# Head-pair attention of batch 0 in another engine order, with moved key-transpose slots, Sin table load, GpSimd squares and V load

## The chip, the cores and the metric

The kernel runs on one core of a Trainium2 chip. The metric is the device time of one execution in microseconds; of several executions the median is given. The core's engines are TensorE (PE in the profile; PEld is its weight load), VectorE (DVE), ScalarE (ACT), GpSimd (POOL) and SyncE (SP). Each works through its own list of instructions in order and waits on semaphores for the others.

## What is computed

Chunked attention, and behind it an MLP with a snake activation, over 4 batches of 768 rows, 8 heads of 64:

```
for c in range(24):                      # chunk 32, left 16, right 8
    k_full = concat(mem_k, k[max(0, 32c-16) : min(768, 32c+40)])   # 8 memory rows first; v likewise
    a = softmax(q_c @ k_full.T / 8)
    out[:, :, 32c:32c+32] = a @ v_full
x = out.transpose(0, 2, 1, 3).reshape(3072, 512)
h = x @ w_in                             # 512 -> 2048
g = h + sin(alpha * h)**2 / (alpha + 1e-09)
result = g @ w_out                       # 2048 -> 512
```

Inputs and output are float32; the kernel multiplies in bf16.

## The kernel before, in words

Three chunks make a window of 96 queries, whose scores are 128 rows of keys: a window's keys, 8 memory keys among them, lie side by side in `kTi`, and the same for values in `vws[b % 2]`. A batch has 8 windows and 4 head pairs, so 32 cells. A unit of attention takes 4 cells. Its steps are: scores (8 matmuls, L266, into a PSUM tile `sc`), exponentials with masks as bias on ACT (L279, into `pt`), PV (8 matmuls, L294, into `ot`), reciprocal and scaling on DVE (L298, L299, into `x_blk`), a transpose on PE (L309) and a copy into `xT` (L312).

For batches 1 to 3 (`burst`) a unit is one window of all head pairs. The last layer of the batch before, held in a generator (`Stream`, matmuls at L439), is woven between the steps. For batch 0 (`first_burst`) there is nothing to weave in, and a unit is half of the windows of one head pair: units 0 and 1 are pair 0, and so on. Its order is written by hand in the string `ORDER`: `k n` and `q n` transpose the keys and queries of pair n on PE (L241) and copy them to `kTi` (DVE, L246 and L252) and `qT` (L259: ACT for pairs 0 and 2, DVE for 1 and 3); `memk` and `memv` place memory keys and values of batch 0 (L147, L141); `s n` is scores and exponentials of unit n; `v n` PV and scaling; `x n` the transpose to `xT`; `z n` is n spin matmuls on zeros (L160), which also precede each transpose inside `turn`. Since every engine takes its instructions in program order, this string sets what each engine does next.

PSUM has eight banks here: three two-bank slots (`big`, for scores, PV and first-layer tiles) and two one-bank slots (`smp`, for spins, batch 0's transposes and second-layer outputs).

After the burst comes the first layer of the batch, 16 tiles `ft` of 128 features (`l1`): 8 matmuls (L382), Sin on ACT (L394, or L391 in two halves), a square, and a fused multiply and add on DVE into `gT` (L411, or L407 in halves). A string of 16 letters says which engine squares: A for ACT (L397), D for DVE (L403), P for GpSimd (L399). The square on DVE and the fused operation of a tile are issued after the next tile's preparations (`finish`). In batch 0 tiles 3, 7 and 11 are split tiles: they use the one-bank slots, so that more tiles are in flight.

Exp and Sin need different tables on ACT, so each change between attention and first layer loads one (ACT_TABLE_LOAD).

GpSimd also issues the loads (q, k, v, weights; they cast to bf16), and copies each head pair of the next batch together (`pair_up`, L215, tile `pr`) for its transposes (L238); in batch 0 some of these copies are DVE's. Batch 1's values are loaded (`load_v(1, ...)`, four issues, L138) from within batch 0's first layer, and its pairs are transposed after it, three matmuls of the last layer between two transposes.

The memory values come as f32 in `memv_f`, once for all batches, and are cast once on ACT (L189) into `memv_st`; `put_memv(b)` copies batch b's to all windows (L141).

Of the kernel before, what the change touches and what calls it, by code (L numbers as in the profile page):

```python
# [11 lines left out]
NEG = -30000.0  # L12
KW = 856
ORDER = (
    "k 0,q 0,memk 0,k 1,s 0,q 1,s 1,memv 0,s 2,k 2,v 0,q 2,s 3,x 0,v 1,k 3,s 4,x 1,q 3,s 5,"
    "z 1,v 2,s 6,x 2,z 1,v 3,s 7,x 3,z 2,v 4,z 2,v 5,x 4,z 1,v 6,x 5,z 1,v 7,x 6,z 1,x 7"
)
BF = mybir.dt.bfloat16
F32 = mybir.dt.float32
# [30 lines left out]
def kernel(  # L50
# [45 lines left out]
    memkT = consts.tile([P, HP, 32], BF, name="memkT")  # L96
    memv_st = consts.tile([P, B, H, D], BF, name="memv_st")
    memk_f = gp.tile([32, H, D], F32, name="memk_f", tag="gT")
    memv_f = gp.tile([P, B, H, D], F32, name="memv_f", tag="gT")
    w_in_sb = consts.tile([P, KT, d_ff], BF, name="w_in_sb")  # L100
    w_out_sb = consts.tile([P, FT, d_model], BF, name="w_out_sb")
    alpha_sb = consts.tile([P, FT], F32, name="alpha_sb")
# [35 lines left out]
            nc.gpsimd.dma_start(dst, src)  # L138

    def put_memv(b):  # L140
        nc.vector.tensor_copy(  # L141
            vws[b % 2][64:72, :, :, 0:D],
            memv_st[64:72, b].unsqueeze(2).to_broadcast([NM, H, NJ, D]),
        )
# [41 lines left out]
    nc.vector.tensor_scalar(  # L186
        out=biasm[:], in0=rows[:, 0:5], scalar1=1.0, scalar2=-NEG, op0=ALU.subtract, op1=ALU.mult)
    nc.scalar.copy(memk_bf[:], memk_f[:])
    nc.scalar.copy(memv_st[64:72], memv_f[64:72])  # L189
    for hp in range(1, HP):  # L190
        load_v(0, 16 * hp, 16 * hp + 16)
    with nc.allow_non_contiguous_dma(reason="alpha transpose load"):
# [32 lines left out]
            return smp.tile([P, 6, P], BF, name="tt_a", tag="sm")  # L225
        return big.tile([P, 6, P], BF, name="tt_b", tag="big")

    def turn(src, hp):

        if src.shape[1] == 6:  # L230
            t = t_tile()
        else:
            z = smp.tile([P, 512], F32, name="z", tag="sm")
            spin(2, z)
            t = z[:].bitcast(BF)[:, 0:6 * P].rearrange("p (r c) -> p r c", r=6)
        for r in range(6):
            if src.shape[1] == 6:
                nc.tensor.transpose(t[:, r, :], src[:, r].rearrange("p e d -> p (e d)"), ident[:])  # L238
            else:
                for e in range(2):  # L240
                    nc.tensor.transpose(t[64 * e:64 * e + 64, r, :], src[:, 2 * hp + e, r, :], ident[:])  # L241
        return t

    def t_k(kb, hp):
        t = turn(kb, hp)
        nc.vector.tensor_copy(  # L246
            kTi[:, hp, 72:72 + 7 * 104].rearrange("p (s c) -> p s c", c=104)[:, :, 0:96]
            .rearrange("p s (a r) -> p s a r", r=6),
            t[:, :, 8:120].rearrange("p r (s a) -> p s a r", a=16),
        )  # L250
        for t0, c0 in ((0, 16), (120, 800)):
            nc.vector.tensor_copy(  # L252
                kTi[:, hp, c0:c0 + 48].rearrange("p (a r) -> p a r", r=6),
                t[:, :, t0:t0 + 8].rearrange("p r a -> p a r"),
            )
# [2 lines left out]
        t = turn(qb, hp)  # L258
        copy(qT[:, hp, :].rearrange("p (a r) -> p a r", r=6), t[:, :, :].rearrange("p r a -> p a r"))  # L259

    def qk_exp(cells):

        sc = big.tile([P, 2, 512], F32, name="sc", tag="big")
        for c, (hp, j) in enumerate(cells):
            for e in range(2):
                nc.tensor.matmul(  # L266
                    sc[:, e, QW * c:QW * c + QW],
                    kTi[64 * e:64 * e + 64, hp, 104 * j:104 * j + P],
                    qT[64 * e:64 * e + 64, hp, QW * j:QW * j + QW],
                )  # L270
        pt = pts[state["n"] % NPT]
        state["n"] += 1
        for m in range(3):
            cols = [((1 if j == 0 else 0), 4, (2 if j == NJ - 1 else 3))[m] for _, j in cells]
            c0 = 0
            for c1 in range(1, 5):
                if c1 < 4 and cols[c1] == cols[c0]:
                    continue
                nc.scalar.activation(  # L279
                    pt[:, 0:H * QW].rearrange("p (g e c) -> p e g c", g=4, e=2)[:, :, c0:c1, 32 * m:32 * m + 32],  # L280
                    sc[:, :, 0:4 * QW].rearrange("p g (e c) -> p g e c", e=4)[:, :, c0:c1, 32 * m:32 * m + 32],
                    ACTF.Exp, bias=biasm[:, cols[c0]:cols[c0] + 1], scale=0.125,
                )
                c0 = c1
        return pt
# [28 lines left out]
    def row(j):  # L314
        return [(hp, j) for hp in range(HP)]

    def burst(b, stream, shares, lag):

        xT = xp.tile([P, KT, S], BF, name="xT")
        ptl, xbl = {}, {}  # L320
        for s in range(NJ + lag + 1):
            n = shares[s] if s < len(shares) else 0
            if s < NJ:
                ptl[s] = qk_exp(row(s))
            stream.take(n // 3, True)
            if 0 <= s - lag < NJ:
                xbl[s - lag] = pv(b, row(s - lag), ptl.pop(s - lag))
            stream.take((n + 1) // 3, True)
            if 0 <= s - lag - 1 < NJ:
                j = s - lag - 1  # L330
                xt(xT[:, :, QW * j:QW * j + QW], *xbl.pop(j))
            stream.take((n + 2) // 3, True)
        return xT

    def first_burst(kq):

        xT = xp.tile([P, KT, S], BF, name="xT")
        cells = [[(u // 2, 4 * (u % 2) + c) for c in range(4)] for u in range(8)]
        ptl, xbl = {}, {}
        for what, n in [t.split() for t in ORDER.split(",")]:  # L340
            n = int(n)
            if what == "k":
                t_k(kq[0], n)
            elif what == "q":
                t_q(kq[1], n, nc.vector.tensor_copy if n in (1, 3) else nc.scalar.copy)
            elif what == "memk":
                mt = smp.tile([P, HP, 32], BF, name="mt", tag="sm")
                for hp in range(HP):
                    nc.tensor.transpose(
                        mt[:, hp, :],  # L350
                        memk_bf[0:32, 2 * hp:2 * hp + 2, :].rearrange("p e d -> p (e d)"),
                        ident[0:32, 0:32])
                nc.vector.tensor_copy(memkT[:], mt[:])
                put_memk(0)
            elif what == "memv":
                put_memv(0)
            elif what == "s":
                ptl[n] = qk_exp(cells[n])
            elif what == "z":
                spin(n)  # L360
            elif what == "v":
                xbl[n] = pv(0, cells[n], ptl.pop(n))
            elif what == "x":
                hf = n % 2
                xt(xT[:, n // 2, HALF * hf:HALF * hf + HALF].rearrange("p (k c) -> p k c", k=KT),
                   *xbl.pop(n), nc.vector.tensor_copy if n < 4 else nc.scalar.copy)
        return xT
# [95 lines left out]
    for i in range(B):  # L463
        gT = gp.tile([P, FT, S], BF, name="gT")
        last = i == B - 1
        at_ft = {2 * n: n for n in range(8)}
        pieces = []
        if not last:
            srcs = [(kq_next[n % 2], n // 2) for n in range(2 * HP)]
        state["pools"] = 1  # L470

        def pair_to(n):
            while len(pieces) < min(n, 2 * HP):
                pieces.append(pair_up(*srcs[len(pieces)], nc.vector.tensor_copy if i == 0 and len(pieces) in (2, 4, 6) else None))

        def piece(n):
            pair_to(n + 3)
            (t_k if n % 2 == 0 else t_q)(pieces[n], n // 2)

        if 0 < i < B - 1:  # L480
            pair_to(2)
        finish = None
        for ft in range(FT):
            sq = ("ADAPADAPDADADAAA" if i == 0 else "ADAAPDADADAPADAD")[ft]
            if 1 <= ft:
                stream.take(3 if last else 2)
            if 0 < i < B - 1 and ft in at_ft:
                piece(at_ft[ft])
            if i == 0 and ft == 8:
                load_v(1, 0, H * NJ)  # L490
            if i == 0 and ft == 13:
                pair_to(2)
            if finish is not None:
                finish()
            finish = l1(i, ft, xT, gT, sq, i == 0 and ft in (3, 7, 11))
        finish()
        stream.add(l2(i, gT, last))
        if not last:
            if i == 0:
                state["pools"], state["t"] = 3, 0  # L500
                stream.take(4)
                for n in range(2 * HP):
                    piece(n)
                    stream.take(3, True)
                put_memv(1)
            if i + 2 < B:
                kq_next = load_qk(i + 2)
            if i == 0:
                xT = burst(i + 1, stream, (5, 5, 5, 4, 4, 4, 4, 4, 3, 3, 3, 3), 3)
            else:  # L510
                xT = burst(i + 1, stream, (16, 8, 6, 6, 6, 5, 5, 5, 5, 5), 1)
            if i + 2 < B:
                put_memk(i + 2)
            stream.take(3)
            if i + 2 < B:
                load_v(i + 2, 0, H * NJ)
                put_memv(i + 2)
# [31 lines left out]
```

## Time and profile before

| | us |
|---|---|
| median of 4 runs | 237.43 (236.72 to 237.66) |
| the profiled execution | 236.15 |
| its span | 234.3 |
| busy: PE / DVE / ACT / POOL | 215.9 / 160.2 / 153.2 / 71.6 |
| first-layer matmuls L382, x488 | 87.3 |
| last-layer matmuls L439, x343 | 93.1 |
| batch 0: first burst until the first first-layer matmul | 27.80 |
| batch 0: first Sin / last Sin of the first layer starts | 29.80 / 52.44 |
| batch 1: first scores / first PV | 61.95 / 67.02 |

Times within the profile count from the span's start. In the rows of busy tenths each digit is the busy share of one of 40 equal slices, and PEclk is the clock that TensorE was granted. In the lines of a timeline stand start, length (of one instruction, or of a merged run of them), engine, source line, operation, output<-input, shapes and count; in brackets, how long the engine was idle before it and what ended that. The ends of matmuls are modelled, and GpSimd's spans are rough.

### The profile page before, as it was taken

To read this page: it belongs to the slowest core of one execution; us is meant where nothing else is said; L and a number is where in the kernel's file an instruction comes from. 1 tells how busy PE (TensorE), PEld (TensorE's weight loads), DVE (VectorE), ACT (ScalarE), POOL (GpSimd) and SP (SyncE) were. 2 spreads that over 40 slices of the span, in tenths; PEclk is the share of its full clock that TensorE was granted. 3 is DMA by queue.
4 is the path that set the end of the run, shared out by engine and by line. 5 is a ranking of instruction groups with operands and counts; after the bars stand their busy time and mean duration, and the time that the engine had idled before them with its cause. 6 is when DMAs were issued, how large, how long until landed. Compare 5 with 4: busy or idle time off the path is not lost.

```text
span 234.3 us, 4546 instructions
## 1 busy us (share of the span) xinstructions
PE 215.9 (92%) x1802; PEld 121.7 (52%) x1831; DVE 160.2 (68%) x287; ACT 153.2 (65%) x244; POOL 71.6 (31%) x84
## 2 busy tenths in 40 slices
PE   7677899969999999998999999998999999899994
PEld 2344555535545565554455656564555555453453
DVE  5488658997847987988557698978566358775110
ACT  3679499875697297899664787779564676880000
POOL 8899603923942115138300115020000020010000
PEclk9999999999999999999999999999999999999999
DMA  7999999999999910019996101000111110101112
GB/s 83 150 174 114 168 205 205 207 192 104 146 222 168 109 45 0 0 49 141 184 154 98 45 0 48 0 8 36 48 48 45 45 49 0 45 0 48 64 71 90
DMA packets 52365, 21.13 MB, mean 90 GB/s; under 512 B 36344, under 2 KB 49400, under 8 KB 52344
## 3 DMA queue, kind: packets, MB, share of 16 engines
q0 software_dynamic: 46128, 14.41, 72.3%
q1 hardware_dynamic: 6216, 6.43, 9.4%
q8 instruction: 14, 0.23, 0.5%
q14 instruction: 7, 0.06, 0.1%
HBM read 28.93 MB, written 6.29 MB: 150 GB/s over the span
## 4 chain that ended last, share of the span: by engine, by line
PE 64%; DVE 17%; issue 7%; ACT 6%; DMA 2%; POOL 1%; POOLq 1%; DVEq 0%; ACTq 0%
PE o L439 30%; PE hT L382 20%; DVE gT L411 6%; PE sc L266 3%; DVE s L403 3%; ACT u L394 3%; DVE x_blk L299 3%; PE ot L294 3%; PE ot L309 2%; DMA q_bf<-in_q_dram 2%; PE tt_a L238 2%; ACT s L397 2%; PE o L428 1%; DVE kTi L246 1%; PE z L160 1%
## 5 line engine op out<-in xcount | busy, mean ns | idle before, releaser
L439 PE MATMUL o<-w_out_sb,gT 128*128 128x512 bf16 x343 | 93.1, 380 | 2.0 <-issue 0.5
L382 PE MATMUL hT<-xT,w_in_sb 128*128 128x384 bf16 x488 | 87.3, 326 | 4.4 <-DVE gT L411 4.2
L411 DVE SCALAR_TENSOR_TENSOR gT<-s,inv_alpha,hT 128x768 bf16<-128x768 f32 x61 | 60.9, 1013 | 24.7 <-ACT s L397 16.7
L394 ACT ACTIVATE u<-hT,alpha_sb 128x768 f32<-128x768 f32 x61 | 54.6, 897 | 25.0 <-PE hT L382 23.9
L382 PEld LDWEIGHTS <-w_in_sb 128*128 128x128 bf16 x512 | 49.3, 98 | 39.6 <-issue 5.9
L279 ACT ACTIVATE pt<-sc,biasm 128x256 bf16<-128x256 f32 (+2 forms) x104 | 39.2, 464 | 14.3 <-PE sc L266 14.0
L439 PEld LDWEIGHTS <-gT 128*128 128x128 bf16 x368 | 31.9, 98 | 26.3 <-DVE gT L411 1.2
L399 POOL TENSOR_TENSOR s<-u 128x768 f32<-128x768 f32 x8 | 11.7, 1465 | 83.5 <-ACT u L394 61.3
L397 ACT ACTIVATE s<-u 128x768 f32<-128x768 f32 x33 | 27.8, 843 | 1.0
L138 POOL DMA_DIRECT2D vw<-in_v_dram x28 | 24.6, 889 | 0.3 <-issue 0.2
L403 DVE TENSOR_TENSOR s<-u 128x768 f32<-128x768 f32 x23 | 23.8, 1037 | 0.6 <-ACT u L394 0.5
L299 DVE TENSOR_TENSOR x_blk<-ot,rinv 96x512 bf16<-96x512 f32 x32 | 22.0, 686 | 1.1
L215 POOL COPY pr<-q_bf 128x768 bf16<-128x768 bf16 x12 | 10.2, 853 | 40.6 <-PE tt_a L238 27.1
L446 DVE COPY o_sb<-o 128x512 f32<-128x512 f32 x12 | 8.3, 689 | 15.5 <-PE o L439 15.4
L448 ACT COPY o_sb<-o 128x512 f32<-128x512 f32 x11 | 6.4, 582 | 17.9 <-PE o L439 17.9
L298 DVE RECIPROCAL rinv<-ot 96x8 f32<-96x8 f32 x32 | 6.4, 201 | 16.1 <-PE ot L294 15.8
L294 PEld LDWEIGHTS <-pt 128*128 128x128 bf16 x256 | 12.0, 97 | 6.3 <-issue 1.3
L294 PE MATMUL ot<-vw,pt 128*128 128x65 bf16 x256 | 13.0, 193 | 0.6 <-DVE xT L312 0.5
L160 PE MATMUL z<-zeros 128*128 128x512 bf16 x31 | 11.1, 456 | 2.5 <-DVE zeros L153 1.2
L266 PEld LDWEIGHTS <-kTi 64*128 64x128 bf16 x256 | 6.8, 94 | 12.3 <-PE ot L309 5.5
L309 PE MATMUL ot<-ident,x_blk 96*128 96x96 bf16 x128 | 10.8, 207 | 2.5 <-DVE x_blk L299 2.3
L238 PEld LDWEIGHTS <-pr 128*128 128x128 bf16 x144 | 10.0, 98 | 5.9 <-DVE pr L215 0.8
(65 smaller groups left out, 155.4 us busy)
## 6 DMA issues: line engine op xcount, KB each, us to landing
out_dram<-o_sb SPq DMA_DIRECT2D x23, 256.0 KB, 2.2
k_bf<-in_k_dram POOLq DMA_DIRECT2D x3, 768.0 KB, 7.6
q_bf<-in_q_dram POOLq DMA_DIRECT2D x3, 768.0 KB, 11.4
vw<-in_v_dram POOLq DMA_DIRECT2D x6, 384.0 KB, 15.6
w_out_sb<-in_moe_w_out_dram POOLq DMA_DIRECT2D x2, 1024.0 KB, 24.5
w_in_sb<-in_moe_w_in_dram POOLq DMA_DIRECT2D x3, 512.0 KB, 9.8
k_bf<-in_k_dram POOLq DMA_DIRECT2D x4, 192.0 KB, 5.1
q_bf<-in_q_dram POOLq DMA_DIRECT2D x4, 192.0 KB, 5.3
```

The lines of the kernel that those rows point to most:

```text
L138: nc.gpsimd.dma_start(dst, src)
L238: nc.tensor.transpose(t[:, r, :], src[:, r].rearrange("p e d -> p (e d)"), ident[:])
L279: nc.scalar.activation(pt[:, 0:H * QW].rearrange("p (g e c) -> p e g c", g=4, e=2)[:, :, c0:c1, 32 * m:32 * m + 32], sc[:, :, 0:4 * QW].re ...
L294: nc.tensor.matmul(otv[:, n // 4, n % 4, :], pt[:, QW * n:QW * n + P], vws[b % 2][:, 2 * hp + n % 2, j, 0:D + 1])
L299: nc.vector.tensor_tensor(out=x_blk[:].rearrange("p (g e) d -> p g e d", g=2), in0=otv[0:QW, :, :, 0:D], in1=rv.unsqueeze(3).to_broadcast( ...
L309: nc.tensor.transpose(xtp[:, kt, :], x_blk[:, 2 * kt:2 * kt + 2, :].rearrange("p e d -> p (e d)"), ident[0:QW, 0:QW])
L382: nc.tensor.matmul(hts[hf][:, 0:HALF], w_in_sb[:, kt, P * ft:P * ft + P], xT[:, kt, HALF * hf:HALF * hf + HALF], start=(kt == 0), stop=(kt ...
L394: nc.scalar.activation(u[:], hT[:, :, 0:HALF], ACTF.Sin, scale=alpha_sb[:, ft:ft + 1])
L397: nc.scalar.activation(s2[:], u[:], ACTF.Square)
L403: nc.vector.tensor_tensor(out=s2[:], in0=u[:], in1=u[:], op=ALU.mult)
L411: nc.vector.scalar_tensor_tensor(out=gv, in0=s2[:], scalar=inv_alpha[:, ft:ft + 1], in1=hT[:, :, 0:HALF], op0=ALU.mult, op1=ALU.add)
L439: nc.tensor.matmul(o[:], gT[:, ft, P * s:P * s + P], w_out_sb[:, ft, :], start=(ft == 0), stop=(ft == FT - 1),)
```

## The change

The order of the first burst is a new string, with scores (`s`) and exponentials (`e`) as separate steps. The memory values come straight after the memory keys; the second unit's scores no longer follow `q 1`; some spins go or move. The transposes of keys of pairs 0 and 1 use a two-bank slot; `turn` spins 3 times for pairs 0 and 1 and once for the others, instead of twice. The cast of memory values is per batch, on DVE for batch 0 and on ACT for the others, and `memv_f` has a buffer of its own. After the last exponentials of the burst a Sin of one column is issued, and the Sin table with it. In batch 0's first layer five squares change engine: 8 and 10 go from D to A, 9 from A to D, 11 and 14 from A to P. Batch 1's first two pair copies stand at tile 8 instead of 13, and the load of its values after the 16 tiles instead of at tile 8.

```diff
 ORDER = (
-    "k 0,q 0,memk 0,k 1,s 0,q 1,s 1,memv 0,s 2,k 2,v 0,q 2,s 3,x 0,v 1,k 3,s 4,x 1,q 3,s 5,"
-    "z 1,v 2,s 6,x 2,z 1,v 3,s 7,x 3,z 2,v 4,z 2,v 5,x 4,z 1,v 6,x 5,z 1,v 7,x 6,z 1,x 7"
+    "k 0,q 0,memk 0,memv 0,k 1,s 0,e 0,z 1,s 1,e 1,q 1,s 2,e 2,v 0,s 3,k 2,x 0,q 2,e 3,v 1,s 4,e 4,"
+    "k 3,x 1,q 3,s 5,e 5,v 2,z 1,s 6,e 6,x 2,v 3,z 1,s 7,e 7,x 3,z 1,v 4,z 1,v 5,x 4,z 1,v 6,x 5,z 1,v 7,x 6,z 1,x 7"
 )
...
-    memv_f = gp.tile([P, B, H, D], F32, name="memv_f", tag="gT")
+    memv_f = consts.tile([P, B, H, D], F32, name="memv_f")
...
     def put_memv(b):
+        (nc.vector.tensor_copy if b == 0 else nc.scalar.copy)(memv_st[64:72, b], memv_f[64:72, b])
         nc.vector.tensor_copy(
...
-    nc.scalar.copy(memv_st[64:72], memv_f[64:72])
...
-    def turn(src, hp):
+    def turn(src, hp, early=False):
...
-            z = smp.tile([P, 512], F32, name="z", tag="sm")
-            spin(2, z)
+            if early:
+                z = big.tile([P, 512], F32, name="zb", tag="big")
+            else:
+                z = smp.tile([P, 512], F32, name="z", tag="sm")
+            spin(3 if hp < 2 else 1, z)
...
-        t = turn(kb, hp)
+        t = turn(kb, hp, hp < 2)
...
             elif what == "s":
-                ptl[n] = qk_exp(cells[n])
+                scl[n] = qk(cells[n])
+            elif what == "e":
+                ptl[n] = exps(cells[n], scl.pop(n))
+                if n == 7:
+                    nc.scalar.activation(rows[:, 0:1], zeros[:, 0:1], ACTF.Sin)
...
-            sq = ("ADAPADAPDADADAAA" if i == 0 else "ADAAPDADADAPADAD")[ft]
+            sq = ("ADAPADAPADAPDAPA" if i == 0 else "ADAAPDADADAPADAD")[ft]
...
             if i == 0 and ft == 8:
-                load_v(1, 0, H * NJ)
-            if i == 0 and ft == 13:
                 pair_to(2)
...
         if not last:
             if i == 0:
+                load_v(1, 0, H * NJ)
                 state["pools"], state["t"] = 3, 0
```

`qk` and `exps` are the two halves of the former `qk_exp`, unchanged; `burst` calls one after the other.

More of the change, by code (lines that the diff above doesn't have):

```diff
@@ L259, in t_q, with qk @@
         copy(qT[:, hp, :].rearrange("p (a r) -> p a r", r=6), t[:, :, :].rearrange("p r a -> p a r"))
-    def qk_exp(cells):
+    def qk(cells):
         sc = big.tile([P, 2, 512], F32, name="sc", tag="big")
@@ L270, in qk_exp, with exps @@
                 )
+        return sc
+    def exps(cells, sc):
         pt = pts[state["n"] % NPT]
@@ L323, in burst @@
             if s < NJ:
-                ptl[s] = qk_exp(row(s))
+                ptl[s] = exps(row(s), qk(row(s)))
             stream.take(n // 3, True)
@@ L338, in first_burst @@
         cells = [[(u // 2, 4 * (u % 2) + c) for c in range(4)] for u in range(8)]
-        ptl, xbl = {}, {}
+        scl, ptl, xbl = {}, {}, {}
         for what, n in [t.split() for t in ORDER.split(",")]:
```

## The prediction

> **What bounds the kernel now.** I read the page's rows of busy tenths first, to see where an engine is not full. One column is 5.86 us.
>
> ```profile
> PE   7677899969999999998999999998999999899994
> DVE  5488658997847987988557698978566358775110
> ACT  3679499875697297899664787779564676880000
> POOL 8899603923942115138300115020000020010000
> PEclk9999999999999999999999999999999999999999
> ```
>
> From column 14 on TensorE is nearly full. In columns 1 to 5 (head-pair attention, to 27.8 us), no engine is full: there a chain of hand-overs sets the time. Columns 6 to 9 (first layer of batch 0) have PE, ACT and DVE all near full. The change works in these two stretches, so I took the timeline of them next.
>
> ```profile
> 6.84 1.89 ACT L189 CAST memv_st<-memv_f 8x2048 bf16<-8x2048 f32 x1 [1.28 <-DMA memv_f<-in_mem_v_dram]
> 8.57 0.50 DVE L147 COPY kTi<-memkT 128x256 bf16<-128x256 bf16 x1
> 8.76 0.80 ACT L259 COPY qT<-z 128x768 bf16<-128x768 bf16 x1
> ...
> 12.21 2.60 ACT L279 ACTIVATE pt<-sc,biasm 128x256 bf16<-128x256 f32 x8 [0.86 <-PE sc L266]
> ...
> 12.92 1.37 DVE L141 COPY vw<-memv_st 8x4096 bf16<-8x4096 bf16 x1
> ...
> 28.50 1.28 ACT L394 ACT_TABLE_LOAD   x1
> 29.80 0.90 ACT L394 ACTIVATE u<-hT,alpha_sb 128x768 f32<-128x768 f32 x1
> ...
> 50.94 1.46 PE L382 MATMUL hT<-xT,w_in_sb 128*128 128x384 bf16 x8 [1.57 <-DVE gT L411]
> ...
> 53.73 0.83 POOL L215 COPY pr<-q_bf 128x768 bf16<-128x768 bf16 x1 [5.55 <-PE tt_b L238]
> ...
> 61.54 2.07 DVE L141 COPY vw<-memv_st 8x4096 bf16<-8x4096 bf16 x1
> ...
> 62.22 1.28 ACT L279 ACT_TABLE_LOAD   x1
> ```
>
> The reader sees: ACT spends 1.89 us on memory values while the first query copy is ready (its transposes end at 8.09); the Sin table is loaded only when everything before it is done; the last first-layer tile waits 1.57 us for DVE; and the same memory-value copy costs 1.37 us once and 2.07 us another time.
>
> The profiled execution took 236.15 us: 234.3 of span and 1.85 around it. It is 0.5% under the runs' median of 237.43. I sum against the profile and carry the difference over.
>
> **1. The first burst.** ACT's 1.89 us copy goes: the first query copy starts at 8.1, not 8.76. The first scores (9.61) then wait for the k 1 transposes in front of them and start about 9.3. Their exps, 1.35 us, start at 9.7. The second scores now follow at once and no longer stand behind q 1, so their exps start at 11.05 instead of 12.21, 1.15 earlier.
>
> That is not the gain of the stage, because DVE gets more to do before k 1. Put_memk ends at 9.07. Then comes a copy of 8x512 values that no row shows: ACT's 32x512 cast of 0.62 bounds it above, DVE's 128x768 bf16 copy of 0.35 (55.17) below; I take 0.45, between, as it reads f32. Then the 8x4096 copy, 1.37 (1.22 to 2.07), the k 1 copies, 1.09 (9.68 to 10.77), and the q 1 copy, 0.96: 9.07 + 0.45 + 1.37 + 1.09 + 0.96 = 12.94. It ended at 12.89, so the third scores win nothing. PV 0 does: it stood behind k 2 (14.39) and now follows them, at 13.3. Its DVE result leaves about 1.7 us earlier, and from there the DVE work interleaves better. The last exps end near 23.0 instead of 23.63 (18.09 + 5.54): 0.6. Behind them, "z 2" becomes "z 1" twice; the second spin of a pair costs 0.60 - 0.38 = 0.22, one of the two hidden by waits for x_blk, so 0.2 to 0.4. The rest (PV, x_blk every 0.85, transpose, copy) keeps its length. hT starts at 26.9 instead of 27.80: **-0.9** (bounds -0.3 with the 2.07 copy and its followers, -1.3).
>
> The other parts cost nothing here. The extra spins before k 0 (0.4 at the cold 0.43 each) lie in the wait for q 0, 7.56, from which k 0 had over 1 us; without that cover they cost 0.4. The two-bank slots of k 0 and k 1 are free by the third scores (k 0's copies ended at 7.46). The DVE copies may hold up GpSimd's issues beside them (13.22 took 1.21 instead of 0.61). q 3 was issued at 10.18 and lands after a median of 5.3, at 15.5; its transposes come near 17.5, so 0.6 later is hidden. The values' own f32 buffer takes no one's place and adds no wait.
>
> **2. The table.** The eight hT matmuls end at 27.80 + 7 x 0.162 + 0.33 = 29.26, the table at 29.78: 0.54 was exposed. Now it is issued after the last exps, near 23.0, where ACT idled 1.71 before the first xT copy (25.34). With the dummy Sin (0.32, by the smallest exp) that is 1.60, and the copies wait for x_blk anyway. **-0.54**; if that idle time were gone, up to 1.28 would come back through the xT copies. [...] In the trace the ACTIVATE starts 1.30 after the load; I use the row.
>
> **3. Squares.** ACT loses one of 0.84 and DVE one of 0.95, GpSimd gains two of 1.47. Tile 11 is the costly one: its square takes 1.47 on GpSimd instead of 0.84 on ACT, and DVE's sum for tile 11 heads DVE's queue; behind it stand the square of 12 and the sums of 12 to 15, and the last hT waits for the sum of 12. u 11 ended at 45.66; 1.44 earlier by items 1 and 2 and 0.8 later by the square that ACT gains among 8 to 10 makes 45.0, the square 46.5. DVE has then sat idle for about 1.1 us, against the 0.95 of the one square fewer that it has by then. Tile 14 takes 0.6 longer but its sum is behind 12 and 13. I take **+0.2** (bounds -0.4, +0.8).
>
> [...]
>
> ```profile
> 84.30 0.83 POOL L215 COPY pr<-k_bf 128x768 bf16<-128x768 bf16 x1 [2.69 <-PE tt_a L238]
> 84.44 1.49 DVE L403 TENSOR_TENSOR s<-u 128x768 f32<-128x768 f32 x1
> ```
>
> A DVE square of 0.95 took 1.49. But under the two GpSimd squares of this stage (35.05, 40.31) lay only sums with one SBUF input, and these stayed 1.01. The new squares meet sums too. [...]
>
> **4. GpSimd's queue.** The V load of batch 1 (four issues, 41.72 to 46.0, 4.29 us) moves behind the square of 14. In front of it now stands that square's wait for u 14; behind it, the three q pair copies and the loads of batch 2. u 14 ended at 50.41; 1.44 earlier and 0.3 for what ACT no longer does makes 48.7, so square 14 ends near 50.2, the issues at 54.5, the q 1 pair at 55.3. Its transposes, at 56.58, would come 1.25 earlier, 55.3: just in time. Each further slip is paid one for one. **+0.1** (0 to +1.5). Landing: the issues took a median of 16.9 us to land, the last at 45.17 + 16.9 = 62.1, queued behind the second-layer weights; these still go first, so the V rows land near 62 to 64, before PV at 66.
>
> **5. Memory values per batch.** Batch 1's 8x512 copy, 0.62 by the nearest row, now stands on ACT between the last query copy and the Exp table (62.22). All exps move by it. PE had some 0.3 of slack there (the second PV at 68.54 starts as the fourth exps end), so **+0.35** (0 to 0.6). DVE waits for that copy; behind it stands nothing before 67.47. In batches 2 and 3 it lies in ACT's idle 4.42 and 1.22 us before u: nothing; without that cover 0.62 each.
>
> Sum: -0.9 - 0.54 + 0.2 + 0.1 + 0.35 = -0.79. The profile's 236.15 becomes 235.4, and the median 237.43 becomes 236.6.
>
> **Rivals.** A difference below 0.3% (0.7 us) can't be told from none.
> [...]
> - *GpSimd's queue becomes the bound: 238.2, slower.* If the V issues meet DVE copies as at 62.54 (2.02 instead of 1.34, so 0.7 each for the long ones), or square 14 is late, q 1's pair is ready 1.6 us late, TensorE stands still and -0.8 becomes +0.8. It decides once the pair copy ends more than 0.85 after 55.3. For: nothing covers that stretch. Against: in the same issues at 41.72 none was stretched.
> - *TensorE cools: 239.* Two spins fewer in all; if the clock fell in the burst, spins and matmuls double (0.43 instead of 0.215). The PEclk row shows no dip near it.
>
> **Chances.** Forecast 42%; returned by the lock, 33%; GpSimd's queue 20%; clock 5%. Faster 0.42, same 0.33, slower 0.25. The range goes from a front gain at its bound (237.43 - 1.6 = 235.8) to the queue rival with 0.1 beyond it, 238.3; the forecast's own case is 235.8 to 236.9.
>
> **What would show it.** Right: hT starts near 26.9, u 0 near 28.4, the table load lies near 23; u 15 comes 1.2 earlier than 52.44; DVE idles about 1 us before tile 11's sums; the Exp load follows a 0.6 us ACT copy. Wrong: the 8x4096 copy lasts 2 us near 10; TensorE waits for a pair copy near 55, or PV near 66 for V.

## The result, and the profile after

The changed kernel takes 236.24 us (median of 37 runs, 235.24 to 238.57), the kernel before beside it 237.27 (56 runs, 236.17 to 239.05). The ratio is 0.9959, with a 95% interval of 0.9944 to 0.9973: 0.4% faster, with an interval that excludes 1 and reaches 0.27% at its weaker end. The prediction was 236.6, in a range of 235.8 to 238.3.

One thing has to be known to read any number below: executions of either kernel fall in groups by the mean clock that TensorE was granted, so parts are compared at full clock (a mean of at least 0.997), and the others, in which the clock dropped for a while, are counted. At full clock the kernel before takes 236.53 (50 of 100 executions beside all the experiments) and the changed one 235.69 (16 of 37): 0.84 less, against the 0.79 of the prediction's sum. With one drop of the clock the changed one takes 236.62 (20 of 37), so a drop costs 0.93; the last execution, at a mean clock of 0.977, took 238.57. The groups below are small: drawing again at random from their executions shows that a difference of two of their medians is uncertain by 0.2 to 0.4, so those of 0.2 are not told from none by the times alone.

The profiled execution took 236.76 us, with a span of 235.0. It is one with a drop. Its rows of busy tenths:

```profile
PE   7967899959989999998999999998999999899994
DVE  5777668878637987988557598978466358875110
ACT  3469699844696387899664887779564676880000
POOL 8889623466852115139210215120000020010000
PEclk9999999989999999999999999999999999999999
```

PEclk has an 8 in the ninth column, and in the same column TensorE's row has a 5: TensorE stands still, and then runs at a lower clock. That is the tail of the first layer of batch 0. The timeline of the same execution (start, length, engine, line, operation, and in brackets the idle time before it and what ended that):

```profile
7.03 0.82 PE L161 MATMUL z<-zeros 128*128 128x512 bf16 x3
...
7.78 0.53 PE L244 MATMUL z<-ident,q_bf 128*64 128x128 bf16 x12
...
9.11 0.42 DVE L141 CAST memv_st<-memv_f 8x512 bf16<-8x512 f32 x1
...
9.56 1.39 DVE L142 COPY vw<-memv_st 8x4096 bf16<-8x4096 bf16 x1
...
12.97 0.34 PE L269 MATMUL sc<-qT,kTi 64*128 64x96 bf16 x8 [1.18 <-DVE qT L262]
13.25 0.42 PE L300 MATMUL ot<-vw,pt 128*128 128x65 bf16 x8
...
23.41 1.28 ACT L368 ACT_TABLE_LOAD   x1
...
27.16 4.07 PE L392 MATMUL hT<-xT,w_in_sb 128*128 128x384 bf16 x24
28.66 0.90 ACT L404 ACTIVATE u<-hT,alpha_sb 128x768 f32<-128x768 f32 x1 [0.82 <-PE hT L392]
...
45.32 1.47 POOL L409 TENSOR_TENSOR s<-u 128x768 f32<-128x768 f32 x1 [0.89 <-ACT u L401]
46.82 1.14 DVE L417 SCALAR_TENSOR_TENSOR gT<-s,inv_alpha,hs 128x384 bf16<-128x384 f32 x2 [1.03 <-POOL s L409]
...
50.00 2.17 PE L392 MATMUL hT<-xT,w_in_sb 128*128 128x384 bf16 x8 [2.32 <-DVE gT L421]
...
63.21 1.22 DVE L142 COPY vw<-memv_st 8x4096 bf16<-8x4096 bf16 x1 [1.36 <-ACT memv_st L141]
```

In the burst the lines fall where the prediction put them: the cast on DVE 0.42 (0.45 taken), the long copy 1.39 (1.37), the third scores at 12.97 (12.94: no gain), PV 0 at 13.25 (13.3). hT starts at 27.16 instead of 27.80, although in this execution the first transposes began 0.77 later than before (6.57 against 5.80). The first two lines show a cost of the new order: the query rows of pair 0 landed at 7.04 (4.8 after their issue at 2.19), but three spins stand in front of their transposes, which start only at 7.78. The Sin table lies at 23.41, and u 0 waits for TensorE alone: 1.50 after hT's start, 2.00 before.

In the tail, DVE idles 1.03 for the square of tile 11, and the last tile's matmuls wait 2.32 instead of 1.57. Then something new: these eight matmuls take 2.17 instead of 1.46. The busy time in stretches of 2 us (length, then PE, PEld, DVE, ACT, POOL, each with its count of instructions, then the granted clock, DMA share and GB/s):

```profile
48.00:50.00 2.00, 0.00 (x1) 0.00 (x1) 1.90 (x3) 1.03 (x2) 0.89 (x1) 1.00 1.24 207
50.00:52.00 2.00, 2.00 (x9) 1.03 (x9) 1.79 (x2) 0.00 (x0) 2.00 (x3) 0.65 1.00 166
52.00:54.00 2.00, 1.78 (x8) 0.90 (x8) 0.00 (x0) 1.74 (x2) 2.00 (x3) 0.50 1.12 77
```

A stretch in which TensorE did nothing is followed by half the clock, from 50.60 for 3.41 us.

### The profile page after: what moved, and what is told of

It reads as the page before. It is cut to its first block, busy times and chain, and to the rows that moved or that the text cites. A ratio compares the mean times of both kernels' runs of the same rounds, so it can differ in the third digit from the quotient of the medians.

```text
span 235.0 us, 4549 instructions
## 1 busy us (share of the span) xinstructions
PE 217.4 (93%) x1802; PEld 122.7 (52%) x1830; DVE 159.4 (68%) x287; ACT 152.5 (65%) x246; POOL 74.2 (32%) x86
## 4 chain that ended last, share of the span: by engine, by line
PE 65%; DVE 16%; ACT 9%; issue 6%; POOL 2%; POOLq 1%; DVEq 0%; ACTq 0%
PE o L449 27%; PE hT L392 22%; DVE gT L421 5%; ACT u L404 3%; PE ot L300 3%; DVE x_blk L305 3%; PE z L161 3%; PE sc L269 3%; PE ot L315 2%; DVE s L413 2%; PE tt_a L241 2%; ACT pt L285 2%; POOL s L409 2%; PE o L438 1%; ACT s L407 1%
## 5 line engine op out<-in xcount | busy, mean ns | idle before, releaser
L409 POOL TENSOR_TENSOR s<-u 128x768 f32<-128x768 f32 x10 | 14.7, 1465 | 85.3 <-ACT u L404 63.6
L407 ACT ACTIVATE s<-u 128x768 f32<-128x768 f32 x32 | 27.0, 843 | 1.0
L413 DVE TENSOR_TENSOR s<-u 128x768 f32<-128x768 f32 x22 | 22.9, 1040 | 0.7 <-ACT u L404 0.5
L215 POOL COPY pr<-q_bf 128x768 bf16<-128x768 bf16 x12 | 10.8, 898 | 35.3 <-PE tt_a L241 24.7
L269 PE MATMUL sc<-qT,kTi 64*128 64x96 bf16 x256 | 11.2, 205 | 3.0 <-DVE qT L262 1.5
```

The costliest lines, as they stand in the source:

```text
L269: nc.tensor.matmul(sc[:, e, QW * c:QW * c + QW], kTi[64 * e:64 * e + 64, hp, 104 * j:104 * j + P], qT[64 * e:64 * e + 64, hp, QW * j:QW * ...
L407: nc.scalar.activation(s2[:], u[:], ACTF.Square)
L409: nc.gpsimd.tensor_tensor(out=s2[:], in0=u[:], in1=u[:], op=ALU.mult)
L413: nc.vector.tensor_tensor(out=s2[:], in0=u[:], in1=u[:], op=ALU.mult)
```

## The experiments

Theory: the parts add up as in the prediction's sum (burst, table, squares, V load, cast), and the new tail loses the clock on top. Rivals: the burst's gain is spent in the tail, the cost of the squares is GpSimd's queue, and the drops have nothing to do with the change. Each kernel was run some 6 to 12 times beside the kernel before; times are medians of all executions, "full" those at full clock, with their number. Where a stage is compared between profiles, I count from the start of batch 0's first hT matmul, since its own time varies between profiles of the same burst by up to 0.9 us (26.87 to 27.76 with the new one).

**The kernel before, unchanged.**

> The kernel before, unchanged, so that the granted clock of each of its executions is seen. Theory 1 (the halved clock is a cost of the changed kernel's longer stall before the last first-layer tile, 2.3 us instead of 1.6): nearly all executions show a clock of 0.998 or more and the times lie close together, within 0.5 us. Theory 2 (the clock falls in the kernel before too, and does as much harm there): some executions near 0.992, about 0.9 us slower than the others.

Measured: 236.84, ratio 1.0004 (0.9981 to 1.0028); full 236.59 (7 of 12). The kernel before loses the clock as well, in 5 executions here and in 50 of the 100 others. So drops are not the change's own. Both of its profiles are without a drop; where its drops lie, no trace of it shows.

**Old squares.**

```diff
-            sq = ("ADAPADAPADAPDAPA" if i == 0 else "ADAAPDADADAPADAD")[ft]
+            sq = ("ADAPADAPDADADAAA" if i == 0 else "ADAAPDADADAPADAD")[ft]
```

> The changed kernel with the former letters for the squares of batch 0. Theory 1: the stall before the last hT falls from 2.3 to about 1.6 us, the clock stays at 1.0, and the median falls by about 0.6 (0.9 us in two executions of three) to 235.6. Theory 2 (the clock does not hang on the squares): same as the changed kernel within 0.3, some executions still near 0.992. If the squares are a gain by themselves, as their authorship of one DVE and one ACT operation less would have it, this is slower by 0.3 or more at the same clock.

Measured: 235.32, ratio to before 0.9942 (0.9921 to 0.9962); all 9 executions at full clock. The new squares cost 0.37 at full clock, and the drops of more than half of the executions besides, together 0.92. The timeline of this kernel:

```profile
49.78 1.46 PE L392 MATMUL hT<-xT,w_in_sb 128*128 128x384 bf16 x8 [1.57 <-DVE gT L421]
...
55.00 0.83 POOL L215 COPY pr<-q_bf 128x768 bf16<-128x768 bf16 x1 [1.60 <-PE tt_a L241]
...
55.28 0.76 DVE L215 COPY pr<-k_bf 128x768 bf16<-128x768 bf16 x1
55.42 0.50 PE L241 MATMUL tt_b<-ident,pr 128*128 128x128 bf16 x6
```

The wait at the last tile is 1.57 again, as before the change, and the q 1 pair copy on GpSimd waits for its slot, not for GpSimd's queue: TensorE goes on at 55.42 without a wait for it.

**Spins into the tail's wait.** The squares stay new; only TensorE is kept busy.

```diff
+            if i == 0 and ft == 15:
+                spin(8)
```

> The changed kernel with 8 spin matmuls (1.7 us at full clock) between the matmuls of first-layer tile 14 and tile 15 of batch 0, inside the 2.3 us stall. Theory 1: the clock is 0.998 or more in all executions and the median is 235.7, 0.6 below the changed kernel's 236.24. Rival (the stall counts, not the clock): same as the changed kernel, 236.2, or slower where the spins wait for their PSUM slot.

Measured: 235.78, ratio 0.9955 (0.9935 to 0.9976); full 235.76 (10 of 12). The drops shrink from 21 in 37 to 2 in 12 while the full-clock time stays (235.69 without spins). So the drops of the changed kernel follow from the idle time in this place, and they are separate from the 0.37. Two executions in 12 still drop; where, no trace shows.

**Sin table late.**

```diff
-                if n == 7:
-                    nc.scalar.activation(rows[:, 0:1], zeros[:, 0:1], ACTF.Sin)
```

> The changed kernel without the early Sin of one column: the table is loaded before the first Sin, as in the kernel before. By the prediction the load is exposed again by 0.54 us at the first Sin, and since ACT, PE and DVE are all near full in that stage, most of it reaches the end: +0.5 us, u 0 at 29.2 instead of 28.7. Rival (slack before the last tile takes it up): below +0.2.

Measured: 236.98, ratio 0.9991 (0.9970 to 1.0013); full 236.26 (5 of 12), so the early table is worth 0.57 there, and 0.54 was the prediction's term. u 0 starts 2.00 after hT again, and the last tile's matmuls 23.19 after it, against 22.84 in the changed kernel: in the profiles the early table is worth 0.35 there and 0.40 at the last output copy. Its profile has a drop too, from 51.38 for 3.41 us, right behind a wait of 2.32 at the last tile.

**Old burst.** The former order, slots, spins and buffer of the values, which are cast once on ACT; table, squares and V load as in the changed kernel.

```diff
-    "k 0,q 0,memk 0,memv 0,k 1,s 0,e 0,z 1,s 1,e 1,q 1,s 2,e 2,v 0,s 3,k 2,x 0,q 2,e 3,v 1,s 4,e 4,"
+    "k 0,q 0,memk 0,k 1,s 0,q 1,s 1,memv 0,s 2,k 2,v 0,q 2,s 3,x 0,v 1,k 3,s 4,x 1,q 3,s 5,"
...
-        (nc.vector.tensor_copy if b == 0 else nc.scalar.copy)(memv_st[64:72, b], memv_f[64:72, b])
...
+    nc.scalar.copy(memv_st[64:72], memv_f[64:72])
```

> The changed kernel with the burst of batch 0 as it was before: the old engine order, k 0 and k 1 transposes in one-bank slots, two spins ahead of each, the memory values cast once on ACT ahead of everything. The early Sin table (behind the last exps), the new squares and the moved V load stay. If the burst is worth what the prediction's step 1 took (0.9 us) and the per-batch cast costs its 0.35, this kernel is 0.55 us slower than the changed one (236.8 against 236.24 over all executions), hT starts near 28.0 and u 0 near 29.5 in a full-clock execution. Rival: the burst's gain in hT's start is lost again before the second layer begins (the tail of the first layer waits for the squares, not for its start); then this kernel is as fast as the changed one or faster by the 0.35 of the cast, 235.9 to 236.2.

Measured: 236.72, ratio 0.9986 (0.9958 to 1.0013); full 236.70 (10 of 12): 1.01 slower at full clock, not 0.55; over all executions 0.48, since only 2 of these 12 have a drop. hT starts at 28.04. Why the drops are so few here, although the last tile's wait is 2.32 as in the changed kernel, stays open. The rival that the burst's gain is spent in the tail falls.

**Memory values cast on DVE in every batch.**

```diff
-        (nc.vector.tensor_copy if b == 0 else nc.scalar.copy)(memv_st[64:72, b], memv_f[64:72, b])
+        nc.vector.tensor_copy(memv_st[64:72, b], memv_f[64:72, b])
```

> The changed kernel with the cast of a batch's memory values on DVE in every batch, not on ACT in batches 1 to 3. If the ACT cast ahead of the Exp table costs what it lasts (0.61 us, less the slack of TensorE there: the prediction's 0.35; the changed profile shows the second PV waiting 0.42 for exps, and no such wait before), this kernel is 0.35 to 0.45 us faster, 235.8 over all executions, and the Exp table of batch 1 starts about 0.6 earlier against the first scores. Rival: the DVE cast (0.42) goes in front of the 8x4096 copy and the vw copies behind it, the wait only changes its engine, and the time stays within 0.1 us of the changed kernel's 236.24.

Measured: 235.71, ratio 0.9946 (0.9918 to 0.9975); full 235.51 (8 of 12), 0.18 under the changed kernel, half of what was expected and, by these few executions, not told from none. Counted from hT, the profiles give more: the last output copy starts 203.64 after hT here and 203.96 in the kernel with the spins, which has the same tail at full clock and the cast on ACT: 0.32. The profile of this run shows the changed tail at full clock, and where the squares cost:

```profile
50.15 1.46 PE L392 MATMUL hT<-xT,w_in_sb 128*128 128x384 bf16 x8 [2.32 <-DVE gT L421]
50.67 4.45 POOL L138 DMA_DIRECT2D vw<-in_v_dram  x4
...
55.12 1.60 POOL L215 COPY pr<-q_bf 128x768 bf16<-128x768 bf16 x2
...
55.65 1.28 DVE L215 COPY pr<-k_bf 128x768 bf16<-128x768 bf16 x1
...
56.01 0.34 PEld L241 LDWEIGHTS <-pr 128*128 128x128 bf16 x6 [0.55 <-POOL pr L215]
```

The q 1 pair copy starts the moment the V issues end, TensorE waits 0.55 for it, and two GpSimd copies now lie back to back beside DVE's key copy, which takes 1.28 instead of 0.76. Counted from hT, the last tile's matmuls start at 22.84 here and at 22.79 with the old squares: 0.05 apart, in spite of the longer wait. Batch 1's first scores start at 34.38 against 33.80: 0.58 apart. The same 0.58 stands between this kernel and the one with the old squares and this cast (34.38 against 33.80; last output copy 203.64 against 203.06). So the loss lies behind the first layer, in GpSimd's queue.

**V load back ahead of tile 8**, the two pair copies behind it.

```diff
             if i == 0 and ft == 8:
+                load_v(1, 0, H * NJ)
                 pair_to(2)
...
-                load_v(1, 0, H * NJ)
```

> The changed kernel with the V load of batch 1 back ahead of tile 8, the pair copies behind it. By the prediction's step 4 (0.1 us for the moved load) it is 0.1 us faster, and no more than 0.3 faster: in the changed profile the q 1 pair copy ends at 55.6, about when its transposes can start. Rival A, GpSimd's queue bounds the way into batch 1: then it is 0.5 to 1.0 faster, 235.3 to 235.7. Rival B, the load issues at tile 8 stand in front of the square of tile 11 and of the pair copies (4.3 us of issues), so the square comes later and it is slower by 0.3 or more, with a longer wait of TensorE at the last first-layer tile.

Measured: 237.76, ratio 1.0007 (0.9976 to 1.0038); full 236.65 (4 of 12): 0.96 slower at full clock, where 0.1 faster was expected. Rival B holds:

```profile
40.46 4.29 POOL L138 DMA_DIRECT2D vw<-in_v_dram  x4
...
46.30 1.48 POOL L409 TENSOR_TENSOR s<-u 128x768 f32<-128x768 f32 x1
47.81 1.14 DVE L417 SCALAR_TENSOR_TENSOR gT<-s,inv_alpha,hs 128x384 bf16<-128x384 f32 x2 [2.26 <-POOL s L409]
...
50.99 1.46 PE L392 MATMUL hT<-xT,w_in_sb 128*128 128x384 bf16 x8 [3.54 <-DVE gT L421]
```

The issues and the pair copies fill GpSimd until 46.3, tile 11's square starts 19.40 after hT (18.16 in the changed kernel), DVE idles 2.26, TensorE 3.54. From hT to the last output copy it is 0.79 more than with the spins (204.75 against 203.96). Eight of 12 executions lose the clock.

**Only tile 11's square back on ACT.**

```diff
-            sq = ("ADAPADAPADAPDAPA" if i == 0 else "ADAAPDADADAPADAD")[ft]
+            sq = ("ADAPADAPADAADAPA" if i == 0 else "ADAAPDADADAPADAD")[ft]
```

> The changed kernel with only the square of tile 11 back on ACT; the square of tile 14 stays on GpSimd and 12's, 9's and 10's engines stay as in the changed kernel. With both squares on the old engines the changed kernel became 0.92 us faster over all executions and 0.37 at full clock. If tile 11 is the costly one, as the prediction says (its sum heads DVE's queue and everything to tile 15 stands behind it), this kernel shows most of that: 235.4 to 235.6 at full clock and hardly a dip of TensorE's clock, DVE's idle time ahead of the sums of 11 gone and the last tile's matmuls waiting 1.4 to 1.8 us rather than 2.3. Rival: the cost lies in tile 14's square, or in the order in which the squares of 9 and 10 changed places; then it stays at 235.7 at full clock and 236.2 over all, with dips in about half of the executions.

Measured: 235.69, ratio 0.9929 (0.9901 to 0.9956); all 9 at full clock. Half right: tile 11's square makes the drops, but its return brings nothing in the median at full clock, and 0.28 in the profile (203.68 from hT to the last output copy, against 203.96 with the spins). The reason that it is not more:

```profile
50.08 1.46 PE L392 MATMUL hT<-xT,w_in_sb 128*128 128x384 bf16 x8 [1.20 <-DVE gT L421]
50.26 1.47 POOL L409 TENSOR_TENSOR s<-u 128x768 f32<-128x768 f32 x1 [6.12 <-ACT u L404]
...
51.67 4.29 POOL L138 DMA_DIRECT2D vw<-in_v_dram  x4
...
56.85 0.34 PEld L241 LDWEIGHTS <-pr 128*128 128x128 bf16 x6 [1.46 <-POOL pr L215]
```

The last tile waits only 1.20 and starts 22.32 after hT, 0.52 earlier than in the changed kernel. But tile 14's square now runs at 50.26 and the V issues, behind it, at 51.67, 23.91 after hT instead of 23.36 (50.67 in the kernel with the cast on DVE): TensorE waits 1.46 for the q 1 pair. Of the 0.52 that the tail wins, 0.27 is left at batch 1's first scores (34.11 after hT against 34.38): GpSimd's queue takes the rest.

**Only tile 14's square back on ACT.**

```diff
-            sq = ("ADAPADAPADAPDAPA" if i == 0 else "ADAAPDADADAPADAD")[ft]
+            sq = ("ADAPADAPADAPDAAA" if i == 0 else "ADAAPDADADAPADAD")[ft]
```

> The changed kernel with only the square of tile 14 back on ACT; tile 11's stays on GpSimd. The other half of the pair. With tile 11's back on ACT the dips were gone and the full-clock time unchanged (235.69), and the V load, behind the square of 14, made TensorE wait 1.46 us for the q 1 pair copy. So here: the 2.3 us wait at the last tile and the dips in about half of the executions stay; the V issues start behind the square of 11, near 46.8 instead of 50.5, and the wait for the q 1 pair copy is gone. At full clock 235.3 to 235.5 if that wait is what the squares cost there; 235.7 if it is the wait at the last tile that costs.

Measured: 235.80, ratio 0.9950 (0.9924 to 0.9976); full 235.50 (7 of 11), 0.19 under the changed kernel. As expected the V issues start at 46.54, the q 1 pair copy no longer waits for GpSimd, the 2.32 wait and the drops (4 of 11) stay. The gain is at the small end of what was expected; in its profile TensorE waited 1.57 at 55.23 for the second-layer weights instead, which no other profile shows, so that one cannot be used for sizes.

**The whole first-layer stage as before**: old squares, V load at tile 8, pair copies at 13.

```diff
-            sq = ("ADAPADAPADAPDAPA" if i == 0 else "ADAAPDADADAPADAD")[ft]
+            sq = ("ADAPADAPDADADAAA" if i == 0 else "ADAAPDADADAPADAD")[ft]
...
             if i == 0 and ft == 8:
+                load_v(1, 0, H * NJ)
+            if i == 0 and ft == 13:
                 pair_to(2)
...
-                load_v(1, 0, H * NJ)
```

> The changed kernel with the whole first-layer stage of batch 0 as it was before: old squares, V load of batch 1 ahead of tile 8, pair copies ahead of tile 13. The new burst, the early Sin table and the per-batch casts stay. Theory: the V load's new place pays (0.95 us, found with the new squares) only because its four issues would otherwise stand in front of the square of tile 11; with the old squares nothing on GpSimd is waited for in that stage, and by the sum of the parts (before 236.55 at full clock, burst -1.0, table -0.57) this kernel takes 235.0 to 235.3 at full clock, no slower than the one with the old squares and the new place (235.32). Rival: the new place is a gain of its own (pair copies free of the queue, V packets off the weights' queue); then it is 0.7 or more slower than 235.32.

Measured: 235.32, ratio 0.9924 (0.9895 to 0.9953); full 235.31 (8 of 9). With the old squares the place of the V load is worth nothing (235.32 with the new place; from hT to the last output copy 203.39 against 203.38). It saves 0.96 only against the new squares in front of which it would stand.

**Old squares and the cast on DVE**, both edits as above.

> A version put together from the parts that paid: new burst, early Sin table, V load in its new place, old squares, and the memory-value cast on DVE in every batch. The two edits gave 0.37 and 0.18 at full clock and, over all executions, the dips too. If they add up, 235.1 at full clock and over all executions, hardly a dip, 0.8% under the kernel before. Rival: the cast's place is covered once batch 1 starts earlier, then 235.3, the time with the old squares alone.

Measured: 235.13, ratio 0.9906 (0.9874 to 0.9939); all 6 at full clock. The cast's gain is the same with the old squares (0.19; 0.18 with the new), and this is the fastest kernel of the study, 1.1 us under the changed one over all executions. Counted from hT, the last output copy starts at 203.06 instead of 203.38: the cast on ACT cost 0.32 in the profiles, as with the new squares.

**Old burst and old squares**, both edits as above.

> The changed kernel with the old burst (old order, one-bank slots, memory values cast once on ACT) and with the old squares; the early Sin table and the V load's new place stay. It closes the square of old and new burst with old and new squares: at full clock new/new 235.69, new/old 235.32, old/new 236.70. If the two add, it takes 236.33 at full clock; if the sum of the parts counted from the kernel before holds (236.54 less 0.57 for the table), 235.97. It also tells where the kernel before loses TensorE's clock (half of its executions show a lower mean clock; with new burst, early table and old squares 1 of 33 did): in about half of the executions here, if the place is the old burst; hardly ever, if the place is the stretch around the late Sin table.

Measured: 236.50, ratio 0.9982 (0.9947 to 1.0016); full 236.30 (8 of 12). Burst and squares add (236.33 expected). But the sum counted from the kernel before failed: table and V load give it 0.23, not 0.57. Its timeline shows why:

```profile
42.49 0.83 POOL L215 COPY pr<-q_bf 128x768 bf16<-128x768 bf16 x1
42.81 1.32 DVE L405 TENSOR_TENSOR s<-u 128x768 f32<-128x768 f32 x1
```

The square that takes 0.95 alone takes 1.32 beside the pair copy that the change moved to tile 8. u 0 starts 0.50 earlier after hT than in the kernel before, but the last tile's matmuls start 23.15 after hT, as before (23.14), against 22.79 with the new burst and old squares, in whose profile the two do not meet: this meeting takes 0.36, all that the early table wins. It does not belong to the old burst alone: in the profile of the old burst with the new squares the copy (42.94) is too early to hold up the square (43.67), and in that of the new burst with tile 11's square back on ACT the two meet (43.31 and 43.40). Four of 12 executions lose the clock, with the old burst, old squares and the table early: so the late table is not needed for the drops of the kernel before.

## Why the prediction was right, step by step

| step | predicted | medians at full clock | profiles, counted from hT |
|---|---|---|---|
| 1 burst | -0.9 | -1.2 (old burst against new, neither with the cast on ACT in batch 1: 236.70 - 235.51, 236.30 - 235.13) | -0.9 (hT itself) |
| 2 table | -0.54 | -0.57 | -0.35 (last tile) |
| 3 squares | +0.2 | +0.37 together with 4, given the new place of the V load | +0.05 (last tile) |
| 4 GpSimd's queue | +0.1 | 0.0 with the old squares | +0.53 (batch 1's first scores, beyond the last tile's 0.05) |
| 5 cast | +0.35 | +0.18 and +0.19 | +0.32 (last output copy) |
| sum | -0.79 | -0.84 (the changed kernel against the one before) | -0.35 |

The place and sign of every step came out; the close agreement of the two sums is in part luck. The measured terms do not add up to their total (-1.2 - 0.57 + 0.37 + 0.19 = -1.21), and a path from kernel to kernel (table and V load -0.23, burst with its cast -0.98, squares +0.37) closes only because each step begins where the last one ended. The profiles tell sizes better: counted from hT, the squares differ by 0.58 and the cast by 0.32 in either of two pairs of kernels. Against them the medians that use the changed kernel's 235.69 are all off to one side: 0.57 for 0.35 to 0.40 (table), 0.37 for 0.58 (squares), 0.18 for 0.32 (cast), 0.96 for 0.79 (V load), 0 for 0.28 (tile 11's square). All five would fit if 235.69 were some 0.2 too low, which the spread of these 16 executions (235.24 to 236.03) allows; against it stands the kernel with the spins, which should take as long and took 235.76. By this estimate, not by a measurement, the change is worth some 0.6 at full clock. The profiles' own sum is lower still, but the profiled executions with the new burst happened to be 0.3 slower, in the mean of ten, than the median of their kernel at as many drops.

**Burst: right, but for the spins.** hT starts at 28.1 in the mean of four profiles with the old burst (27.80 to 28.44) and at 27.2 in ten with the new one (26.87 to 27.76): 0.9. The chain on DVE that forbids the third scores a gain came out to 0.03. The 2.07 behind the weaker bound (the long copy beside load issues) did not come: 1.39. All of the burst hangs on the start of the q 0 transposes: hT follows 20.24 to 20.26 later in the four old profiles and 19.33 to 19.53 later in the ten new ones. In the kernel before they start when their rows land:

```profile
7.56 0.53 PE L241 MATMUL z<-ident,q_bf 128*64 128x128 bf16 x12 [0.69 <-DMA q_bf<-in_q_dram]
```

The prediction held the extra spins to be covered by this wait. They are not in four of the ten new profiles: the granted clock there became full only at 6.23 to 7.01, the spins before it took 0.43 each, and the q 0 transposes start 0.68 to 0.81 after their rows landed, against 0.04 in all the others. No kernel with the new order and fewer spins in front of q 0 was run. (Nor are there two spins fewer in all: 25 became 24.)

**Table: right in place, the size uncertain.** The trace's idle time was the measure, and u 0 does start 0.5 earlier after hT; 0.35 of it reaches the last tile in the profiles, and 0.57 is the difference of the medians. The Sin starts 1.30 after the load here as well (23.41 and 24.71).

**Squares: right in mechanism, a little dear.** The prediction set DVE's wait for tile 11's square against the one square fewer that DVE has to do, and let the last tile pay 0.2. DVE did idle 1.03 (1.1 predicted), and the last tile did wait longer (2.32 against 1.57). But a wait is not a delay: TensorE had run that much ahead, and the last tile's matmuls start only 0.05 later. With tile 11's square on ACT the other new letters even gain 0.47 (22.32 after hT against 22.79 with the old squares); tile 11's takes 0.52 back.

**GpSimd's queue: the term that was mis-sized.** Step 4 had the q 1 pair copy "just in time", done at 55.3, and took +0.1. No run shows that 0.1 as a term of its own: where a moved pair copy met tile 9's square, the square stayed at 0.95 and the copy took 0.97 instead of 0.82 (changed profile), or the square took 1.55 (tile 11's square back on ACT). In the full-clock profile with the cast on DVE the V issues ended at 55.12, not 54.5, and the copy near 55.9, and TensorE waited 0.55 for it: one of the prediction's own signs of being wrong. The copy's lateness, with the two GpSimd copies that then meet DVE's, comes to 0.53 there. This is the mechanism of the rival on GpSimd's queue, at a third of its price. Put together, steps 3 and 4 were 0.3 and measured 0.58 in the profiles, 0.37 in the medians.

**Cast: right.** DVE's wait (1.36) and the 0.61 copy ahead of the Exp table are in the trace as described, and 0.32 in two pairs of profiles is close to the 0.35; the medians give 0.18 and 0.19.

**What the prediction did not see: the clock.** It gave a rival in which TensorE cools in the burst 5%, because the PEclk row shows no dip. The row is of one execution; half of the executions of the kernel before have one or more. In the changed kernel 21 of 37 do; both profiles with a drop, its own and that of the late table, have it in the tail. In the medians two things of about equal size therefore nearly cancel: the drops that the new tail brings (236.24 over all, 235.69 at full clock) and those that the kernel before had elsewhere (237.27 and 236.53). So the forecast of the medians (236.6 against 236.24) owes something to that. Where the drops are in the kernel before stays open. For the burst speaks that they survive with old burst and early table (4 of 12) and are 1 of 33 with the new burst when tile 11 is squared on ACT; against it, that only 2 of 12 have one with the old burst and the new squares. No trace shows one there. TensorE idles up to 0.52 to 0.54 of 3.41 us near 10 us with the old burst, at most 0.44 anywhere in the new burst; both are less than the 0.57 that passed without a drop.

## What to carry to other kernels

A longer wait of an engine in the trace is not yet a delay (2.32 instead of 1.57 us at the last tile here, and its matmuls 0.05 later): compare the time at which its next work starts, counted from a common event, before a cost is put on it. Work that is moved to an idle engine's queue costs what stands behind it in that queue (0.53 us here at batch 1's first scores), and the value of a place in the queue depends on its neighbours: the same moved load was worth nothing or 0.96 us. A row of granted clock from one execution does not exclude a drop; here a stretch in which TensorE idled for 0.68 of 3.41 us stood ahead of both drops that a profile shows, and eight spins in it were the cheap test (2 drops in 12 executions instead of 21 in 37). When the times of a few executions scatter by more than the effect, stages counted from a common event in the profiles can still tell its size: here the same edit gave the same 0.32 or 0.58 in two pairs of kernels.

## What the runs showed of the hardware

In the changed profile full clock lasts from 6.23 to 50.60, 44.37 us, then half clock for 3.41, then full again for 180.91; in eleven profiles, the kernel before's among them, full clock lasts 228.69. These lengths are 13, 53 and 67 times 3.413. From them I estimate that the clock changes only on a grid of 3.413 us that runs through the execution; no run shows the grid itself. I cut 13 profiles into windows on it and took TensorE's idle share in each. The two windows ahead of the drops had 0.68, every window without a drop behind it 0.57 or less (the drop after the last matmul, left aside). A wait of 2.32 us gives a share of 0.68 only if one window holds all of it; in the profile of the kernel with the cast on DVE, where the grid cuts it, the share is 0.52, and no drop follows. This would explain why the same kernel drops in one execution and not in the next, and why the old tail, whose wait of 1.57 can reach 0.51 at most, does not. It rests on two drops; whether a limit lies between 0.57 and 0.68, no run shows.

Where a DVE square and a GpSimd pair copy overlapped in batch 0's first layer, the one that started later took longer: where the DVE square came first (changed kernel, 42.79 and 43.46) it stayed at 0.95 and the pair copy took 0.97 instead of 0.82; where a pair copy had started 0.32 earlier (old burst and old squares) or 0.09 (tile 11's square back on ACT), the square took 1.32 or 1.55.
